# Permuted tokens, 512-column groups over all batches and a hand-set order in an attention and channel-mix kernel

## The chip, the cores and the metric

The kernel runs on one core of one Trainium2 chip. The metric is the device time of one execution in microseconds (us). Most executions of one kernel agree within about 1%; a run more than 1.5% above the fastest run of the same kernel is marked slow, and only fast runs enter a comparison. PE is the matrix engine (PEld its weight loads), DVE the vector engine, ACT the scalar engine, POOL the engine that issues the casting loads, SP the one that issues the stores.

## The reference

```python
def _attn_ref(q, k, v, g_norm):                       # (8, 8, 576, 64): batch, head, token, dim
    kv = np.einsum('bhsd,bhse->bhde', k, v)
    out = np.einsum('bhsd,bhde->bhse', q, kv)
    rms = np.sqrt(np.mean(out * out, axis=-1, keepdims=True) + 1e-06)
    return out / rms * g_norm

def _moe_ref(x, mu_k, mu_r, w_k, w_v, w_r):           # x: (8, 576, 512); w_k (512, 1024), w_v (1024, 512), w_r (512, 512)
    x_prev = x shifted by one token, zero first
    xk = mu_k * x + (1 - mu_k) * x_prev
    xr = mu_r * x + (1 - mu_r) * x_prev
    k = np.maximum(xk @ w_k, 0)
    return sigmoid(xr @ w_r) * ((k * k) @ w_v)
```

The output of the attention, heads side by side, is the x of the channel mix. All is float32 outside; inside, the matmuls are bf16.

## The kernel before

One batch at a time, 576 tokens in four chunks of 128 and one of 64. While the channel mix of batch b runs, the attention of batch b+1 is put in at four places. Every load moves pieces of one head of one token, 64 elements. The order of instructions is left to a scheduler, which here kept close to the order of the program.

```python
    def emit_partC_st(a):                       # the normalization's 1/rms, by Ln and Exp
        for half in range(2):
            ps_st = ps_tile("ps_st", [H, SH])
            # ... four matmuls with a selector sum the squares of each head ...
            nc.scalar.activation(out=st_sb, in_=ps_st, func=AF.Ln, bias=eps[:H], scale=1.0 / HD)
            nc.scalar.activation(out=rrms[half], in_=st_sb, func=AF.Exp, scale=-0.5)

    for b in range(B):
        a = b + 1
        emit_loads(b + 2)
        if a < B: emit_partA(a)                 # transposes of q (ps_qt), copies by ACT
        emit_moe_km(b, 0); emit_moe_km(b, 1)    # ps_km, relu by ACT, square by DVE
        emit_moe_r(b)                           # ps_r, sigmoid by ACT
        if a < B: emit_partB(a)                 # kv (ps_kv), u = q kv (ps_u), copies by ACT, squares by DVE
        emit_moe_v(b, 0)                        # ps_v, product by DVE, store
        if a < B: emit_partC_st(a)              # above
        emit_moe_v(b, 1)
        if a < B: emit_partC_rr(a)              # ps_rr, products, difference, blends by DVE
        emit_moe_v(b, 2); emit_moe_v(b, 3); emit_moe_v(b, 4)
```

Of the kernel before, what the change touches and what calls it, by code (L numbers as in the profile page):

```python
# [15 lines left out]
def kernel(  # L17
# [13 lines left out]
    nc = tc.nc  # L31
# [4 lines left out]
    SH = S // 2  # L36
    NHP = H // 2
    NFC = F // 128

    tok_chunks = []  # L40
    t0 = 0
    while t0 < S:
        sz = min(128, S - t0)
        tok_chunks.append((t0, sz))
        t0 += sz
    NTC = len(tok_chunks)

    const = ctx.enter_context(tc.tile_pool(name="const", bufs=1))
    stage = ctx.enter_context(tc.tile_pool(name="stage", bufs=4))
    inp = ctx.enter_context(tc.tile_pool(name="inp", bufs=3))  # L50
    work = ctx.enter_context(tc.tile_pool(name="work", bufs=1))
    psum = ctx.enter_context(tc.tile_pool(name="psum", bufs=8, space=bass.MemoryType.PSUM))

    def ps_tile(name, shape, dtype=FP32):
        return psum.tile(shape, dtype, tag="ps", name=name)

    ident = const.tile([128, 128], BF16, name="ident")
    ident4 = const.tile([4, 4], FP32, name="ident4")
    make_identity(nc, ident)
    make_identity(nc, ident4)  # L60
# [4 lines left out]
    sel8 = const.tile([128, 8 * NHP], BF16, name="sel8")  # L65
    nc.vector.memset(sel8, 0.0)
    for hp in range(NHP):
        for e in range(2):
            nc.vector.memset(sel8[64 * e:64 * e + 64, 10 * hp + e:10 * hp + e + 1], 1.0)

    selg = const.tile([H, C], BF16, name="selg")
    nc.vector.memset(selg, 0.0)
    g_row = g_norm.rearrange("(o d) -> o d", o=1)
    for h in range(H):
        nc.gpsimd.dma_start(out=selg[h:h + 1, HD * h:HD * h + HD], in_=g_row)

    kv_sb = [const.tile([128, 128], BF16, name=f"kv{hp}") for hp in range(NHP)]
    for hp in range(NHP):
        nc.vector.memset(kv_sb[hp], 0.0)

    mu_raw_k = const.tile([NHP, 128], FP32, name="mu_raw_k")
    mu_raw_r = const.tile([NHP, 128], FP32, name="mu_raw_r")
    nc.sync.dma_start(out=mu_raw_k, in_=moe_mu_k.rearrange("(j p) -> j p", p=128))
    nc.sync.dma_start(out=mu_raw_r, in_=moe_mu_r.rearrange("(j p) -> j p", p=128))
    mu_sb = const.tile([128, 2 * NHP], FP32, name="mu_sb")
    for idx, raw in enumerate((mu_raw_k, mu_raw_r)):
        ps_mu = ps_tile("ps_mu", [128, NHP])
        nc.tensor.matmul(ps_mu, raw, ident4, start=True, stop=True)
        nc.scalar.copy(out=mu_sb[:, NHP * idx:NHP * idx + NHP], in_=ps_mu)

    w_k_sb = [const.tile([128, F], BF16, name=f"w_k{i}") for i in range(NHP)]
    w_r_sb = [const.tile([128, C], BF16, name=f"w_r{i}") for i in range(NHP)]
    w_v_sb = [const.tile([128, C], BF16, name=f"w_v{i}") for i in range(NFC)]
    w_stage = {}

    def emit_w_dma(tag, src, i, ncols):
        st = stage.tile([128, F], FP32, tag="stage", name=f"stg_{tag}{i}")
        nc.sync.dma_start(out=st[:, :ncols], in_=src[128 * i:128 * i + 128, :])
        w_stage[(tag, i)] = st[:, :ncols]

    def emit_w_cast(tag, dst_list, i, eng):
        src = w_stage.pop((tag, i))
        if eng is nc.scalar:
            eng.copy(out=dst_list[i], in_=src)
        else:
            eng.tensor_copy(out=dst_list[i], in_=src)

    qT_sb = [work.tile([128, S], BF16, name=f"qT{hp}") for hp in range(NHP)]
    xT = [work.tile([128, S + 1], BF16, name=f"xT{hp}") for hp in range(NHP)]
    for hp in range(NHP):  # L110
        nc.vector.memset(xT[hp][:, 0:1], 0.0)
    uT_sb = {}
    sqT = {}
    for hp in range(NHP):
        for half in range(2):
            uT_sb[(hp, half)] = work.tile([128, SH], BF16, name=f"uT{hp}_{half}")
            sqT[(hp, half)] = work.tile([128, SH], BF16, name=f"sqT{hp}_{half}")
    st_sb = work.tile([H, SH], FP32, name="st_sb")
    rrms = [work.tile([H, SH], BF16, name=f"rrms{i}") for i in range(2)]
    xkT = [work.tile([128, S], BF16, name=f"xkT{hp}") for hp in range(NHP)]  # L120
    xrT = [work.tile([128, S], BF16, name=f"xrT{hp}") for hp in range(NHP)]
    dT_dve = work.tile([128, S], BF16, name="dT_dve")
    sqkT = [work.tile([128, S], BF16, name=f"sqkT{fc}") for fc in range(NFC)]
    relu_tmp = [work.tile([128, SH], BF16, name=f"relu{fc}") for fc in range(NFC)]
    sig = [work.tile([128, C], BF16, name=f"sig{ci}") for ci in range(NTC)]
    out_sb = [work.tile([128, C], FP32, name=f"out_sb{ci}") for ci in range(NTC)]

    inp_tiles = {}

    def emit_loads(b):  # L130
        if b >= B:
            return
        d = {}
        for name, src in (("q", q), ("k", k), ("v", v)):
            srcb = src[b].transpose([1, 0, 2])
            lst = []
            for ci, (t0, sz) in enumerate(tok_chunks):
                t = inp.tile([128, C], BF16, tag=f"{name}{ci}", name=f"{name}{ci}")
                nc.gpsimd.dma_start(out=t[:sz], in_=srcb[t0:t0 + sz])
                lst.append(t)  # L140
            d[name] = lst
        inp_tiles[b] = d

    def emit_partA(a):
        tiles = inp_tiles[a]["q"]
        for hp in range(NHP):
            ps_qt = ps_tile("ps_qt", [128, S], BF16)
            for ci, (t0, sz) in enumerate(tok_chunks):
                nc.tensor.transpose(  # L149
                    ps_qt[:, t0:t0 + sz],  # L150
                    tiles[ci][:sz, 128 * hp:128 * hp + 128],
                    ident[:sz, :sz],
                )
            nc.scalar.copy(out=qT_sb[hp], in_=ps_qt)  # L154

    def emit_partB(a):
        ktiles = inp_tiles[a]["k"]
        vtiles = inp_tiles[a]["v"]
        for hp in range(NHP):
            ps_kv = ps_tile("ps_kv", [128, 128])  # L160
            for ci, (t0, sz) in enumerate(tok_chunks):
                nc.tensor.matmul(  # L162
                    ps_kv,
                    ktiles[ci][:sz, 128 * hp:128 * hp + 128],
                    vtiles[ci][:sz, 128 * hp:128 * hp + 128],
                    start=(ci == 0),
                    stop=(ci == NTC - 1),
                )
            for e in range(2):
                sl = slice(64 * e, 64 * e + 64)  # L170
                nc.vector.tensor_copy(out=kv_sb[hp][sl, sl], in_=ps_kv[sl, sl])  # L171
        for half in range(2):
            for hp in range(NHP):
                ps_u = ps_tile("ps_u", [128, SH])
                nc.tensor.matmul(
                    ps_u,
                    kv_sb[hp],
                    qT_sb[hp][:, SH * half:SH * half + SH],
                    start=True,
                    stop=True,  # L180
                )
                ut = uT_sb[(hp, half)]
                nc.scalar.copy(out=ut, in_=ps_u)  # L183
                nc.vector.tensor_mul(out=sqT[(hp, half)], in0=ut, in1=ut)

    def emit_partC_st(a):
        for half in range(2):
            ps_st = ps_tile("ps_st", [H, SH])
            for hp in range(NHP):
                nc.tensor.matmul(  # L190
                    ps_st,
                    sel8[:, 8 * hp:8 * hp + 8],
                    sqT[(hp, half)],
                    start=(hp == 0),
                    stop=(hp == NHP - 1),
                )
            nc.scalar.activation(out=st_sb, in_=ps_st, func=AF.Ln,  # L197
                                 bias=eps[:H], scale=1.0 / HD)
            nc.scalar.activation(out=rrms[half], in_=st_sb, func=AF.Exp, scale=-0.5)  # L199

    def emit_blend(hp, eng, dT):
        xcur = xT[hp][:, 1:S + 1]
        xprev = xT[hp][:, 0:S]
        eng.tensor_tensor(out=dT, in0=xcur, in1=xprev, op=ALU.subtract)
        eng.scalar_tensor_tensor(out=xkT[hp], in0=dT, scalar=mu_sb[:, hp:hp + 1],  # L205
                                 in1=xprev, op0=ALU.mult, op1=ALU.add)
        eng.scalar_tensor_tensor(out=xrT[hp], in0=dT, scalar=mu_sb[:, NHP + hp:NHP + hp + 1],
                                 in1=xprev, op0=ALU.mult, op1=ALU.add)
# [142 lines left out]
```

## Time and profile before

| | before |
|---|---|
| time, median | 316.5 us |
| first channel-mix matmul | 46.9 us; in a row, without waits, from 54.0 |
| period of a middle batch | 34.2 us (83.5 to 117.7) |
| PE busy | 80% of the span |
| ACT table loads | 41, each 1.283 us |

The page's lines below give each engine's busy time and its share of the span, then rows of 40 equal slices of the span (a digit is tenths; PEclk is the clock granted to PE in tenths of full speed), then one DMA queue's packets, and two groups of ACT's instructions with their count, busy us and mean ns.

```profile
PE 251.3 (80%) x1508; PEld 137.9 (44%) x1508; DVE 186.6 (59%) x479; ACT 173.5 (55%) x343; POOL 110.4 (35%) x144
PE   1023568995999599987999599959998699959994
PEclk9999956998999979997999899997999799988999
q0 software_dynamic: 112768, 14.16, 74.3%
L199 ACT ACT_TABLE_LOAD x16 | 20.5, 1283 | 0.3
L197 ACT ACT_TABLE_LOAD x16 | 20.5, 1283 | 0.3
```

PE is the busiest engine, but slices with a 5 or 6 come back (the 10th, 14th, 23rd, 27th, 32nd and 36th), about one period of 34.2 us apart (4.3 slices; one dip is split between the 18th and 19th), and the clock dips to 7 or 8 in the same slice or the next. The chain of waits shows why. Each line has the start, the length and what the chain was on:

```profile
99.92 0.40 ACT uT_0_149 L183
...
102.45 1.28 ACT L197
103.75 0.49 ACT st_sb L197
104.30 1.26 issue
105.55 0.44 ACT rrms_166 L199
106.01 1.28 ACT L197
107.31 0.49 ACT st_sb L197
107.82 1.28 ACT L199
109.11 0.45 ACT rrms_167 L199
109.61 1.01 PE ps_rr L214 x7
110.62 7.09 PE ps_v L261 x24
```

From 99.9 to 109.6 the span hangs on ACT. Four of the pieces are loads of an activation table (the lines with an ACT line number and no tile; the second of the four, at 104.30, goes under "issue"). In this program Ln and Exp are taken from different tables: each switch between them has a load of 1.28 us (16 loads at the line of Ln, 16 at that of Exp). PE has only the matmuls of two chunks to do meanwhile. The stretches below (length, then busy us of each engine, granted clock, DMA) show a whole period and its end:

```profile
83.50:117.70 34.20, 30.41 (x189) 16.77 (x189) 22.61 (x58) 21.15 (x42) 12.58 (x15) 0.95 1.04 94
110.00:117.70 7.70, 7.70 (x31) 3.03 (x29) 7.70 (x16) 0.00 (x0) 0.00 (x0) 0.78 0.57 45
```

### The profile page before, as it was taken

To read this page: it belongs to the slowest core of one execution; us is meant where nothing else is said; L and a number is where in the kernel's file an instruction comes from. 1 tells how busy PE (TensorE), PEld (TensorE's weight loads), DVE (VectorE), ACT (ScalarE), POOL (GpSimd) and SP (SyncE) were. 2 spreads that over 40 slices of the span, in tenths; PEclk is the share of its full clock that TensorE was granted. 3 is DMA by queue.
4 is the path that set the end of the run, shared out by engine and by line. 5 is a ranking of instruction groups with operands and counts; after the bars stand their busy time and mean duration, and the time that the engine had idled before them with its cause. 6 is when DMAs were issued, how large, how long until landed. Compare 5 with 4: busy or idle time off the path is not lost.

```text
span 314.5 us, 4358 instructions
## 1 busy us (share of the span) xinstructions
PE 251.3 (80%) x1508; PEld 137.9 (44%) x1508; DVE 186.6 (59%) x479; ACT 173.5 (55%) x343; POOL 110.4 (35%) x144
## 2 busy tenths in 40 slices
PE   1023568995999599987999599959998699959994
PEld 1012234652574237532665247424754266425641
DVE  3100559565974398366856497439836686649712
ACT  2211861975277907792397627790688339760830
POOL 7589989999533705090406400000000000000000
PEclk9999956998999979997999899997999799988999
DMA  7999999999991959299496901010200010010213
GB/s 211 274 185 146 142 212 105 141 142 185 168 117 12 164 41 148 14 113 106 86 75 45 173 34 53 0 67 2 85 2 33 33 70 17 0 69 18 67 41 111
DMA packets 120359, 29.14 MB, mean 93 GB/s; under 512 B 113672, under 2 KB 113680, under 8 KB 120336
## 3 DMA queue, kind: packets, MB, share of 16 engines
q0 software_dynamic: 112768, 14.16, 74.3%
q1 hardware_dynamic: 7568, 14.69, 13.7%
q8 instruction: 12, 0.20, 0.2%
q14 instruction: 11, 0.09, 0.1%
HBM read 33.56 MB, written 9.44 MB: 137 GB/s over the span
## 4 chain that ended last, share of the span: by engine, by line
PE 60%; ACT 21%; DMA 8%; issue 4%; DVE 4%; POOL 2%; DVEq 0%; POOLq 0%
PE ps_km L232 19%; PE ps_v L261 18%; PE ps_r L248 11%; ACT L197 7%; PE ps_kv L162 4%; PE ps_qt L149 4%; ACT L199 3%; DMA q_203<-in_q_dram 3%; PE ps_rr L214 3%; DMA q_207<-in_q_dram 3%; ACT st_sb L197 3%; DMA v_231<-in_v_dram 2%; ACT rrms_167 L199 1%; ACT rrms_166 L199 1%; ACT uT_0_149 L183 1%
## 5 line engine op out<-in xcount | busy, mean ns | idle before, releaser
L154 ACT COPY qT_137<-ps_qt 128x576 bf16<-128x576 bf16 x8 | 5.1, 639 | 62.8 <-PE ps_qt L149 62.8
L232 PE MATMUL ps_km<-xkT_168,w_k_121 128*128 128x288 bf16 x128 | 36.7, 296 | 0.3 <-DVE xT_143 L221 0.3
L232 PE MATMUL ps_km<-xkT_169,w_k_122 128*128 128x288 bf16 x128 | 36.4, 296 | 0.3 <-DVE xkT_169 L205 0.3
L232 PE MATMUL ps_km<-xkT_170,w_k_123 128*128 128x288 bf16 x128 | 34.1, 289 | 0.0
L171 DVE CAST kv_102<-ps_kv 64x64 bf16<-64x64 f32 x16 | 3.5, 222 | 49.5 <-PE ps_kv L162 49.4
L214 PE MATMUL ps_rr<-rrms_167,selg 8*128 8x288 bf16 x32 | 9.4, 314 | 26.2 <-ACT rrms_167 L199 26.2
L232 PE MATMUL ps_km<-xkT_171,w_k_124 128*128 128x288 bf16 x128 | 28.6, 286 | 0.7 <-DVE xkT_171 L205 0.6
L240 ACT ACTIVATE relu_185<-ps_km 128x288 bf16<-128x288 f32 x16 | 7.2, 451 | 29.3 <-PE ps_km L232 29.3
L214 PEld LDWEIGHTS <-selg 8*128 8x128 bf16 x64 | 6.1, 96 | 38.0 <-issue 36.5
L199 ACT ACT_TABLE_LOAD x16 | 20.5, 1283 | 0.3
L197 ACT ACT_TABLE_LOAD x16 | 20.5, 1283 | 0.3
L221 DVE TENSOR_TENSOR xT_141<-uT_1_151,ps_rr 128x288 bf16<-128x288 bf16 x8 | 3.7, 458 | 24.9 <-PE ps_rr L214 24.9
L261 PE MATMUL ps_v<-w_v_129,sqkT_177 128*128 128x512 bf16 (+1 forms) x40 | 17.1, 428 | 0.0
L261 PE MATMUL ps_v<-w_v_130,sqkT_178 128*128 128x512 bf16 (+1 forms) x40 | 16.9, 424 | 0.0
L261 PE MATMUL ps_v<-w_v_131,sqkT_179 128*128 128x512 bf16 (+1 forms) x40 | 16.9, 423 | 0.0
L261 PE MATMUL ps_v<-w_v_132,sqkT_180 128*128 128x512 bf16 (+1 forms) x40 | 16.9, 423 | 0.0
L261 PE MATMUL ps_v<-w_v_133,sqkT_181 128*128 128x512 bf16 (+1 forms) x40 | 16.9, 423 | 0.0
L261 PE MATMUL ps_v<-w_v_134,sqkT_182 128*128 128x512 bf16 (+1 forms) x40 | 16.9, 423 | 0.0
L261 PE MATMUL ps_v<-w_v_135,sqkT_183 128*128 128x512 bf16 (+1 forms) x40 | 16.8, 421 | 0.0
L261 PE MATMUL ps_v<-w_v_136,sqkT_184 128*128 128x512 bf16 (+1 forms) x40 | 16.1, 403 | 0.0
L248 PE MATMUL ps_r<-w_r_125,xrT_172 128*128 128x512 bf16 (+1 forms) x40 | 15.4, 384 | 0.0
L248 PE MATMUL ps_r<-w_r_126,xrT_173 128*128 128x512 bf16 (+1 forms) x40 | 15.2, 379 | 0.0
(429 smaller groups left out, 754.0 us busy)
## 6 DMA issues: line engine op xcount, KB each, us to landing
out_dram<-out_sb_198 SPq DMA_DIRECT2D x8, 256.0 KB, 3.1
out_dram<-out_sb_199 SPq DMA_DIRECT2D x8, 256.0 KB, 3.3
out_dram<-out_sb_200 SPq DMA_DIRECT2D x8, 256.0 KB, 2.0
out_dram<-out_sb_201 SPq DMA_DIRECT2D x8, 256.0 KB, 2.6
out_dram<-out_sb_202 SPq DMA_DIRECT2D x8, 128.0 KB, 2.4
stg_k_263<-in_moe_w_k_dram SPq DMA_DIRECT2D x1, 512.0 KB, 3.4
stg_k_266<-in_moe_w_k_dram SPq DMA_DIRECT2D x1, 512.0 KB, 5.1
stg_k_269<-in_moe_w_k_dram SPq DMA_DIRECT2D x1, 512.0 KB, 6.4
```

Source lines behind the costliest of these rows:

```text
L149: nc.tensor.transpose(ps_qt[:, t0:t0 + sz], tiles[ci][:sz, 128 * hp:128 * hp + 128], ident[:sz, :sz],)
L154: nc.scalar.copy(out=qT_sb[hp], in_=ps_qt)
L162: nc.tensor.matmul(ps_kv, ktiles[ci][:sz, 128 * hp:128 * hp + 128], vtiles[ci][:sz, 128 * hp:128 * hp + 128], start=(ci == 0), stop=(ci == ...
L171: nc.vector.tensor_copy(out=kv_sb[hp][sl, sl], in_=ps_kv[sl, sl])
L197: nc.scalar.activation(out=st_sb, in_=ps_st, func=AF.Ln, bias=eps[:H], scale=1.0 / HD)
L199: nc.scalar.activation(out=rrms[half], in_=st_sb, func=AF.Exp, scale=-0.5)
L214: nc.tensor.matmul(ps_rr, selg[:, 128 * hp:128 * hp + 128], rrms[half], start=True, stop=True,)
L221: nc.vector.tensor_mul(out=xT[hp][:, 1 + SH * half:1 + SH * half + SH], in0=uT_sb[(hp, half)], in1=ps_rr,)
L232: nc.tensor.matmul(ps_km, w_k_sb[cc][:, 128 * fc:128 * fc + 128], xkT[cc][:, SH * hk:SH * hk + SH], start=(cc == 0), stop=(cc == NHP - 1),)
L240: nc.scalar.activation(out=rt, in_=ps_km, func=AF.Relu)
L248: nc.tensor.matmul(ps_r[:sz], xrT[cc][:, t0:t0 + sz], w_r_sb[cc], start=(cc == 0), stop=(cc == NHP - 1),)
L261: nc.tensor.matmul(ps_v[:sz], sqkT[fc][:, t0:t0 + sz], w_v_sb[fc], start=(fc == 0), stop=(fc == NFC - 1),)
```

## The change

The intent as given: tokens permuted so that a load moves runs of 1.5 KB; channel mix in 9 groups of 512 columns over all batches instead of 8 batches of 576; an order set by hand, with the attention between the units of channel-mix matmuls. The core of the diff, cut:

```diff
-                nc.gpsimd.dma_start(out=t[:sz], in_=srcb[t0:t0 + sz])
+                    nc.gpsimd.dma_start(
+                        out=inp_tiles[(n, b)][:, hs, :],
+                        in_=src[n][b, hs].rearrange("h (p j) d -> p h (j d)", j=NJ),   # token = 6 p + j: runs of 6 tokens
+                    )
     ... weights: float32 loads on SP and casts on three engines -> casting loads on POOL's queue, behind batch 0 ...
+    ctx.enter_context(tc.manual_schedule())
     ... transposes, kv, u, stat and rr on parts of the PE array: 64 x 64 outputs, 32-row and 32-column tiles ...
+            if half == 1:
+                nc.scalar.preload_act_table_set("natural_log_exp_and_others")
+            nc.scalar.activation(out=ln, in_=ps, func=AF.Ln, bias=eps, scale=1.0 / HD)
+            nc.scalar.activation(out=st["rs"][:, cs], in_=ln, func=AF.Exp, scale=-0.5)
     ...
+    def front(b, g, slots):                     # after unit slots[i] of group g
+        at(g, slots[0], (a["kv"], [0, 1, 2, 3]))
+        for hp in range(NHP):
+            at(g, slots[1 + hp], (a["transposes"], hp))
+    def rest(b, g, s0):
+        for hp in range(NHP):
+            at(g, s0 + hp, (a["u"], hp), (a["squares"], hp))
+        at(g, s0 + 5, (a["stat"], 1), (a["stat"], 0))
+        at(g, s0 + 8, (a["xmul"], 1))
+        at(g, s0 + 9, (a["xmul"], 0))
+        at(g, s0 + 10, (a["diff"],))
+        for hp in range(NHP):
+            at(g, s0 + 11 + hp // 2, (a["blend"], xk, 0, hp))
+            at(g, s0 + 13 + hp // 2, (a["blend"], xr, NHP, hp))
+    front(1, 0, [0, 1, 2, 3, 4])
+    rest(1, 0, 5)
+    for b in range(2, B):
+        front(b, b - 2, [15, 16, 17, 18, 19])
+        rest(b, b - 1, 2)
```

A group has 20 units of four matmuls: 8 of k (ps_km), 4 of r (ps_r), 8 of v (ps_v); group 0 has r first.

## The prediction

> **What bounds it now.** The chain of waits gives PE 60% of the span, ACT 21%, loads 8%. Three parts:
> - Start, 54 us: the first channel-mix matmul (ps_km) starts at 53.96, after loads until 30.8 us, then attention of batch 0 through ACT and DVE. The loads move 128-byte pieces (112,768 packets); the timeline shows POOL issuing them without a break, 0.87 us for 1024 pieces, 0.71 for 512, 0.55 for one: issue is the limit.
> - Eight batches. In the chain ps_km takes 7.95 us, ps_r 4.43, ps_v 40 matmuls at 0.2215 = 8.87: 21.25 us. Attention's PE work is about 6.9 us (ps_qt 1.85, ps_kv 1.95, ps_u 1.1, ps_st and ps_rr 1 each). Yet the period is 34.2 us (83.47 to 117.71): about 5 us idle, since PE waits for an ACT chain (eight copies, then Ln, Exp, Ln, Exp with 1.28 us table loads), and some 1.5 us lost at a clock of 0.78 after it (stretches table, 110 to 117.7).
> - Tail 4.3 us.
>
> **Removed.** The 64-token fifth chunk, whose matmuls cost a full 0.22 us: 720 matmuls of 512 columns x 0.2215 = 159.5 us against 170, -10.5. The exposed chain: attention is spread between matmul units, so idle and throttle mostly go: about -38 us over seven batches. ACT table loads, 41 to about 17 (-31 us of ACT, off the critical path once attention is). Weight casts on three engines. Loads in 768-byte pieces become DMA-bound.
>
> **Added.** 48 transposes of 96 columns and 48 kv matmuls of 64 columns per batch, instead of 20 + 20 of 128. The trace shows 57 ns per load-and-matmul pair at 128 columns; I estimate 45 to 55 ns: 4.8 us against 3.8. ps_u, ps_st, ps_rr use part of the array each, so should overlap: about 1.7 us instead of 3.1. But changing the tile shape costs about 0.09 us: in ps_qt the step to 64 rows and back starts 0.15 and 0.13 us apart instead of 0.057. [...] About 24 changes per batch x 0.09 = 2 us. Sum about 8 us per batch, 56 for seven (before 48).
>
> **Start.** Batch 0 is 3.5 MB of reads, alone at first; POOL's pace before was 270 GB/s of reads, so I assume 300: q lands at about 14 us. Then transposes 3, u 3.5, stat 3, DVE products, difference and four xr blends 9: first ps_r at about 33 us. Then PE must wait for batch 1's k, v, q, queued behind 5.2 MB of weights: 12.3 MB / 300 GB/s puts q at about 43 us, hence about 5 us of stall in group 0.
>
> **Sum.** 33 + 5 + 159.5 + 56 + tail 3.5 + small waits 3 = 260 us. DVE (about 165 us) and ACT (about 145) stay under PE.
>
> Predicted 260 us, range 243 to 280. Chances: faster 0.97, within 2% 0.02, slower 0.01.
>
> **What would show it.** First ps_r near 33 us. PE 90% or more after 45 us, clock near 1.0. Wide matmuls 0.216 to 0.222 us apart. Group period about 25.5 us for middle groups, 17.7 for the last. PE's waits: batch 1's kin and qin in group 0, little later. About 17 table loads; about 20,000 packets.
>
> **What would make it wrong.** Narrow-tile pairs costing 80 to 100 ns (weight loads not hidden): +20 us. DVE falling behind between units 10 and 16 (12 us of its work against 7 of PE) so that PSUM buffers run out: +2 to 3 us a group. Loads faster than 300 GB/s: -8 us.

## The result, and the profile after

| | before | after |
|---|---|---|
| time, median | 316.5 us | 251.9 us |
| ratio, 95% interval | | 0.793 (0.790 to 0.797) |
| first channel-mix matmul | 46.9 us (in a row from 54.0) | 27.1 us |
| period in the middle | 34.2 us per 576 tokens | 24.5 us per 512 tokens |
| PE busy | 80% | 87% |
| ACT table loads | 41 | 16 |

A ratio is the mean time of one kernel's fast runs over that of the kernel before's in the same rounds, so it is not quite the ratio of the medians. Where I give a difference in us between two versions below, it is the difference of their ratios times 316.5 us.

The page after, the lines that answer to those above:

```profile
PE 218.7 (87%) x1746; PEld 93.2 (37%) x1746; DVE 154.6 (62%) x302; ACT 136.0 (54%) x252; POOL 23.6 (9%) x38
PE   0284369969998999899989998999899989999992
PEclk9997559995999999999999999999999999999999
q0 software_dynamic: 20960, 16.78, 44.1%
GB/s 82 182 208 207 203 203 204 203 81 54 206 182 0 42 183 226 2 45 179 230 2 55 206 197 0 56 114 0 3 83 85 4 0 85 87 9 159 1 55 113
```

PE's row stands at 8 or 9 from the 11th slice to the last but one, and the clock at 9 (90% or more) from the 11th on. The q0 packets fell from 112,768 to 20,960 (with the weights now among them). The last row counts written bytes: through slices 3 to 8 the loads write 203 to 208 GB/s, and since they turn float32 into bf16 they read about twice that (over the whole run 33.56 MB read from HBM against 16.78 MB that q0 wrote). The chain of waits in a middle group:

```profile
75.63 0.60 ACT relu L222
76.24 1.28 ACT L176
77.54 0.51 ACT ln L177
78.07 0.44 ACT rs L178
78.51 0.40 ACT ln L177
78.93 0.44 ACT rs L178
79.40 1.28 ACT L232
80.69 0.61 ACT sig L232
81.34 3.61 PE ps_v L242 x16
```

The chain still runs through the Ln and Exp step, but that step has one table load in place of four (the second one here, at 79.40, brings back the table of the sigmoid; the whole switch takes 1.3 us, from the end of the relu at 76.23 to Ln at 77.54), and PE had r units to do beside it: PE's own wait ahead of ps_v at 81.34 is 0.55 us (the timeline), where it was 3.3 us. The stretches show group 0, a middle group and one of the last two groups, which have no attention in them:

```profile
27.10:66.70 39.60, 33.94 (x305) 13.88 (x306) 21.36 (x40) 16.63 (x32) 3.83 (x5) 0.77 1.01 160
66.70:91.20 24.50, 23.79 (x210) 9.87 (x210) 19.94 (x38) 16.11 (x30) 2.31 (x3) 1.00 0.56 97
210.90:228.20 17.30, 17.30 (x82) 7.84 (x80) 8.66 (x17) 7.10 (x12) 0.00 (x0) 1.00 0.29 78
```

A middle group has 0.7 us of idle PE left; the next ones are the same to 0.1 us. Group 0 takes 39.6 us at a mean clock of 0.77. PE's timeline there, with the wait in brackets, shows the two waits inside it (the 3.49 us in the first line lie ahead of group 0):

```profile
27.12 2.79 PE L229 MATMUL ps_r<-w_r,xr 128*128 128x512 bf16 x4 [3.49 <-DVE xr L202]
33.18 1.49 PE L141 MATMUL ps_kv<-vin,kin 96*64 96x64 bf16 x48 [3.27 <-DMA vin<-in_v_dram]
...
53.94 0.39 PE L242 MATMUL ps_v<-w_v,sqk 128*128 128x512 bf16 x1 [1.95 <-DVE sqk L223]
```

The one at 33.18 is the wait for batch 1's loads. The one at 53.94 is a wait for the last square, whose relu stood in ACT's queue behind the whole Ln and Exp step: in ACT's timeline the table load starts at 49.80 and that relu at 52.84, with Ln, Exp, Ln and Exp between them.

The low clock in the second half of group 0 (0.51 from 55.8 to 62.7 us) belongs to this profile and need not come with the waits: in the profiles of e1_pieces, e3_bybatch, e5_statlate, e7_both and e8_best below the clock row stands at 9 there, and four wide matmuls between two visits of attention take 0.97 us in e1_pieces and e5_statlate (1.81 here at 56.9), in e1_pieces behind a wait for the last square as here (its chain goes through that square at 60.16 us). Ahead of the first ps_km the rows of those profiles say 9 as well, but matmuls are slow there as in this one (clock 0.50 from 21.7 to 38.8 us): four ps_r take 1.89 us at 34.60 here and at 43.10 in e1_pieces. From the first ps_km of group 0 to the first of group 1 it is 26.1 us in this profile and 23.4 us in that of e1_pieces, with the same order at full clock. So lengths of group 0 can be compared only from the first ps_km on, and between profiles with the same clock there.

So where did 65 us come from? The span before is 54 us until ps_km runs in a row, 256 us of batches and a tail of about 4 us. After, it is 27.1 us of start, 39.6 us of group 0, 144.3 us for six groups, 34.5 us for the last two and 4.7 us of tail. The profile alone cannot say which part of a many-part change bought what. The experiments can.

### The profile page after: what moved, and what is told of

Read it like the earlier page. It is cut to its first block, busy times and chain, and to the rows that moved or that the text cites. A ratio compares the mean times of both kernels' runs of the same rounds, so it can differ in the third digit from the quotient of the medians.

```text
span 250.2 us, 4403 instructions
## 1 busy us (share of the span) xinstructions
PE 218.7 (87%) x1746; PEld 93.2 (37%) x1746; DVE 154.6 (62%) x302; ACT 136.0 (54%) x252; POOL 23.6 (9%) x38
## 3 DMA queue, kind: packets, MB, share of 16 engines
q0 software_dynamic: 20960, 16.78, 44.1%
HBM read 33.56 MB, written 9.44 MB: 172 GB/s over the span
## 4 chain that ended last, share of the span: by engine, by line
PE 69%; ACT 15%; DMA 12%; issue 1%; DVE 1%; POOL 1%; DVEq 0%; POOLq 0%
PE ps_v L242 26%; PE ps_km L219 26%; DMA vin<-in_v_dram 9%; PE ps_r L229 5%; PE ps_qt L125 4%; PE ps_u L159 4%; ACT L176 4%; ACT L232 3%; PE ps_kv L141 3%; DMA kin<-in_k_dram 3%; ACT ln L177 3%; ACT rs L178 2%; ACT relu L222 2%; ACT sig L232 1%; DVE out_sb L247 1%
## 5 line engine op out<-in xcount | busy, mean ns | idle before, releaser
L242 PE MATMUL ps_v<-w_v,sqk 128*128 128x512 bf16 x288 | 70.0, 387 | 5.3 <-ACT sig L232 3.3
L219 PE MATMUL ps_km<-xk,w_k 128*128 128x512 bf16 x288 | 68.9, 380 | 0.0
L222 ACT ACTIVATE relu<-ps_km 128x512 bf16<-128x512 f32 x72 | 42.9, 597 | 28.9 <-PE ps_km L219 24.4
L223 DVE TENSOR_TENSOR sqk<-relu 128x512 bf16<-128x512 bf16 x72 | 30.3, 425 | 35.5 <-ACT relu L222 35.3
L229 PE MATMUL ps_r<-w_r,xr 128*128 128x512 bf16 x144 | 37.3, 400 | 3.9 <-DVE xr L202 3.5
L242 PEld LDWEIGHTS <-sqk 128*128 128x128 bf16 x288 | 26.2, 98 | 37.7 <-issue 7.7
L219 PEld LDWEIGHTS <-w_k 128*128 128x128 bf16 x288 | 25.2, 98 | 32.3 <-issue 6.5
L247 DVE TENSOR_TENSOR out_sb<-ps_v,sig 128x512 f32<-128x512 f32 x36 | 24.2, 686 | 16.7 <-PE ps_v L242 16.7
L161 ACT CAST uT<-ps_u 128x288 bf16<-128x288 f32 x64 | 22.1, 413 | 0.0
L190 DVE TENSOR_TENSOR xT_133<-uT,ps_rr 128x288 bf16<-128x288 bf16 x32 | 12.3, 449 | 8.9 <-PE ps_rr L187 8.8
L190 DVE TENSOR_TENSOR xT_134<-uT,ps_rr 128x288 bf16<-128x288 bf16 x32 | 12.3, 449 | 6.7 <-PE ps_rr L187 6.7
L125 PEld LDWEIGHTS <-qin 96*64 96x64 bf16 x384 | 11.1, 119 | 14.3 <-issue 12.3
```

Of the source, the lines that this page charges most:

```text
L125: nc.tensor.transpose(ps[64 * e:64 * e + 64, NP * j:NP * j + NP], qin[:, 2 * hp + e, HD * j:HD * j + HD], ident[:NP, :NP],)
L161: nc.scalar.copy(out=st["uT"][:, hp, cs], in_=ps)
L190: nc.vector.tensor_mul(out=xT[:, hp, NP + HS * half:NP + HS * half + HS], in0=st["uT"][:, hp, cs], in1=pss[hp])
L219: nc.tensor.matmul(ps, w_k_sb[:, cc, 128 * fc:128 * fc + 128], xk[:, cc, G * g:G * g + G], start=(cc == 0), stop=(cc == NHP - 1))
L222: nc.scalar.activation(out=rt, in_=ps, func=AF.Relu)
L223: nc.vector.tensor_mul(out=sqk[g][:, fc, :], in0=rt, in1=rt)
```

## The experiments

Theory at the outset, from the prediction: the order set by hand hides the ACT chain and so makes the largest part of the gain; table loads matter little once attention is spread out. Rivals: the table loads themselves; the long load runs; the wide groups.

### One part undone at a time

**e1_pieces.** Tokens in natural order, loads in pieces of 64 elements, as before; all else as changed.

```diff
-                        in_=src[n][b, hs].rearrange("h (p j) d -> p h (j d)", j=NJ),
+                        in_=src[n][b, hs].rearrange("h (j p) d -> p h j d", j=NJ),
-            nc.vector.tensor_copy(out=xT[:, :, 1:NP], in_=xT[:, :, S:S + NP - 1])     # and in1 of diff and blend one column back
-            dst = out[b].rearrange("(p j) c -> j p c", j=NJ)[j, p:p + cnt]
+            dst = out[b][c:c + cnt]
```

> The changed kernel with tokens in their natural order: the loads go back to pieces of 64 elements (256 bytes read, 128 written), everything else stays. Theory (long runs matter only while loads bound the kernel, that is at the start): batch 1 lands some 9 us later than at 33 us, so +6 to +12 us (258 to 264), and the middle groups keep their period of 24.5 us. Rival (the long runs are a main cause of the gain): +20 us or more, with loads also late in the middle groups.

Measured: 256.1 us median, ratio 0.807 (0.802 to 0.813): 4.4 us slower than the change. The window of expectation began at 6. In the trace kv of batch 1 starts at 38.3 us (33.2 with long runs) and a middle group still takes 24.5 us (70.8 to 95.3), although the loads now are 118,419 packets in all against 26,771. The written rate during the start falls from about 204 to 140 to 180 GB/s in most slices. So the runs are worth something only where loads hold PE up, at the start; the rival falls.

**e2_place** and **e2b_place.** The old placement of the attention steps, in the changed kernel. The two are the same program.

```diff
-    front(1, 0, [0, 1, 2, 3, 4]) ... rest(b, b - 1, 2)
+    for b in range(1, B):
+        a, g = steps[b], b - 1
+        for hp in range(NHP):
+            at(*((g - 1, 19) if g else (0, 3)), (a["transposes"], hp))
+        at(g, 11, (a["kv"], [0, 1, 2, 3]))
+        for hp in range(NHP):
+            at(g, 11, (a["u"], hp), (a["squares"], hp))
+        at(g, 13, (a["stat"], 1), (a["stat"], 0))
+        at(g, 15, (a["xmul"], 1), (a["xmul"], 0), (a["diff"],))      # then the xk and xr blends, also at 15
```

> The changed kernel with the attention steps put where the kernel before has them (transposes ahead of the group, kv and u as a block after the last k or r unit, stat after v chunk 0, products, difference and blends after v chunk 1). Theory (the hand-set order carries the largest part of the gain): per group about 6 us of idle PE plus up to 2 us at a low clock, +40 to +56 us (292 to 308). Rival (the order is worth little; fewer and wider matmuls and table loads made the gain): under +10 us.

> The old placement of the attention steps in the changed kernel once more, since its four times fell into 258 and 264 to 266. If the order is worth about 6 us most fall near 258; if about 13, near 265. Theory: the middle period is 27.2 us in the profiled run against 24.5, seven times, of which the shorter group 0 gives some back, so most near 264.

Measured: of eight times three are fast (257.9, 258.1 and 255.9, mean 257.3 us) and five are marked slow (262.6 to 265.6). By the fast ones the old placement costs about 5 us over the changed kernel's median, where I expected 40 to 56; even the slow ones lie only 11 to 14 us above it. The theory I began with falls: with one table load in the Ln and Exp step, the old coarse placement hides nearly as much as the fine one. In the fast profile PE's remaining waits are 0.9 us a batch for the products that give PSUM buffers (where PE writes its results) back and 0.5 us for kv. The slow profile has the same waits, and a lower clock in its groups (0.94 on average against 1.00 in most groups of the fast one); since only slow runs show that, I draw nothing from it. My second expectation, that most runs fall near 264, came out as two and two and settles nothing.

**e3_bybatch.** Eight groups of one batch: k in halves of 288 columns, r and v in chunks of 128, 128, 128, 128 and 64 tokens.

```diff
-    G = 512
-    NG = B * S // G
+    G = S
+    NG = B
+        m = min(128, G - 128 * ci)               # in unit_r and unit_v; unit_k loops over two halves of 288
```

> The changed kernel with 8 groups of one batch each: k in halves of 288 columns, r and v in four chunks of 128 tokens and one of 64. Theory: wide matmul work rises from 155.5 to about 166 us, all on PE's critical path: +10 to +14 us (262 to 266). Rival (the waits between have room for it): under +3 us.

Measured: 256.8 us, ratio 0.809 (0.805 to 0.813): 4.9 us slower, between theory and rival. The extra matmul work is real: a batch takes 27.5 us in the middle and 20.8 us at the end without attention, so eight batches have 166 us of wide matmuls against 155. But only 4.9 of these 11 us show. In the middle a batch is 3.0 us longer than a group, for 3.5 us more of wide matmuls; PE's wait for ACT is 0.37 us there instead of 0.55. Group 0 is no longer than the change's (38.9 against 39.6 us), but this profile has the full clock from the first ps_km on and the change's has not, so how much of the rest its waits hide is not shown.

**e4_tables.** Only the preload line taken out.

```diff
-            if half == 1:
-                nc.scalar.preload_act_table_set("natural_log_exp_and_others")
```

> The changed kernel without the preload of the table that holds both Ln and Exp: 40 table loads instead of 16, 3.85 us more of ACT in each stat step. Theory (PE already waits 0.55 us a group for the sigmoid behind the stat step, so each added us of ACT there shows): +20 to +30 us (272 to 282). Rival (four PSUM buffers absorb it): under +6 us.

Measured: 291.9 us, ratio 0.920 (0.914 to 0.925): 40 us slower, more than the theory's 20 to 30. The chain of waits of this run:

```profile
107.97 0.60 ACT relu L220
108.58 1.28 ACT L175
...
110.40 1.28 ACT L176
...
112.15 1.28 ACT L175
...
113.97 1.28 ACT L176
...
115.72 1.28 ACT L230
117.02 0.61 ACT sig L230
117.66 4.43 PE ps_v L240 x10
```

Five table loads stand where the changed kernel has two. A period is 30.9 us (99.04 to 129.95) against 24.5: 6.4 us more for 3.85 us of loads. PE is idle for 5.3 us of such a period (0.7 in the change) and busy for 25.6 us (23.8 in the change) with the same matmuls. The stretches of the same run show the rest:

```profile
106.00:114.00 8.00, 5.13 (x32) 2.10 (x32) 3.04 (x8) 7.49 (x12) 0.00 (x0) 1.00 0.24 37
114.00:118.00 4.00, 2.01 (x10) 0.71 (x10) 2.24 (x7) 3.96 (x6) 0.00 (x0) 0.72 0.00 0
118.00:122.00 4.00, 4.00 (x10) 1.48 (x10) 1.96 (x3) 1.08 (x3) 0.00 (x0) 0.50 0.02 4
```

PE is idle for 4.9 of 12 us, in waits of at most 1.51 us, and then its clock is halved: between 118 and 122 us it does 10 wide matmuls at 0.44 us each, not 0.216. So here a wait for ACT is paid twice, once as a wait (4.6 us more of it in a period) and once as slow matmuls behind it (1.8 us); in the middle groups of the change, with 0.7 us of idle PE, the clock is 1.00. In the whole run the mean clock is 0.92.

### The same part alone, in the kernel before

**b1_tables** and **b2_tables** (the same program twice). One preload per batch ahead of Ln and Exp. So that the preload stays where it is put, ACT alone is held to the order of the program.

```diff
+    ctx.enter_context(tc.manual_schedule(engines={mybir.EngineType.Activation}))
     def emit_partC_st(a):
+        nc.scalar.preload_act_table_set("natural_log_exp_and_others")
         for half in range(2):
```

PE's and DVE's instructions are the same, one for one and in the same order, as in the kernel before. On ACT, besides 24 table loads gone, the four casts of w_r move behind the first Ln and Exp step.

> The kernel before with one table preload per batch ahead of Ln and Exp (17 table loads instead of 41); ACT keeps its program order so that the preload stays in place, PE's and DVE's orders are the same instruction for instruction. Theory (the table loads in the stat step are the largest single cause of the gain, also without the new order): 3 x 1.28 us leave the chain that PE waits for in each batch, and PE's clock holds: -27 to -40 us (277 to 290). Rival (the loads cost much only in the new order, which has little else to wait for): under -12 us.

> The kernel before with one table preload per batch once more, for a profile at full clock: 275 to 280 us, the period of a middle batch 29.3 us or less where it was 34.2, and no stretch of low clock in it. If the gain were made elsewhere (start or end), the period would stay near 34.

Measured: 277.5 us, ratio 0.870 (0.862 to 0.879), and 276.6 us, ratio 0.870 (0.862 to 0.879) the second time: 41 us faster than the kernel before, just above what the theory said. (One more run of b1_tables, 323.1 us, had a mean granted clock of 0.77; it is marked slow and not used.) The stretches of two periods of b2_tables:

```profile
74.20:103.40 29.20, 28.85 (x186) 16.32 (x188) 21.91 (x58) 17.30 (x39) 25.87 (x32) 1.00 2.16 171
103.40:132.50 29.10, 28.88 (x186) 16.34 (x188) 21.81 (x57) 17.30 (x39) 12.43 (x16) 1.00 1.09 102
```

The period is 29.1 us where it was 34.2, PE is idle for 0.3 us of it, and the clock is 1.00. Six periods of 5 us make 30 us. Most of the rest is the start: ps_km runs in a row from 45.3 us instead of 54.0; 3.85 us of these 8.7 are the loads in the Ln and Exp step of batch 0. In this run the last v load of batch 0 also landed 4 us earlier (26.8 instead of 30.8), which the moved casts may have caused; I did not test that. So some 36 of the 41 us are the table loads: all but the 4.9 us of the start that they do not explain.

### Undoing all but the preload

**e9_allthree.** The edits of e1, e2 and e3 together; preload, load order and the use of parts of the array kept.

> Natural token order, groups by batch and the old placement together, in the changed kernel with its table preload and its load order kept. Theory (the parts add up): +4.2, +4.9 and +6 to +13 over the changed kernel, 267 to 274, which is near the kernel before with the preload (277.5); the rest of the difference is the start. Rival (the parts hide each other's waits): under 263.

Measured: 285.5 us, ratio 0.898 (0.892 to 0.903): 33 us slower than the change, and slower than the kernel before with the preload. The parts neither add up (theory) nor hide each other (rival); together they cost more than twice the sum of the single ones, 4.4 + 5 + 4.9. A period is 30.4 us (107.0 to 137.4) where e3 alone has 27.5, and its chain goes through DVE's products, difference and blends straight to the first ps_km of the next batch. My reading, argued from these numbers and not tested further: each part undone alone is half hidden in a wait that stays (group 0, or the 0.55 us of a middle group); undone together, nothing is left to hide in.

### Can the remaining waits go?

**e5_statlate.** The Ln and Exp step behind the last unit whose relu or sigmoid PE needs (in group 0 one unit later, in middle groups four), and what follows by as much (the last blends at most to unit 19).

```diff
+    def rest(b, g, s0, st=5):                    # d = st - 5 is added to every later slot
-        at(g, s0 + 5, (a["stat"], 1), (a["stat"], 0))
+        at(g, s0 + st, (a["stat"], 1), (a["stat"], 0))
+    rest(1, 0, 5, st=6)   ...   rest(b, b - 1, 2, st=9)
```

> The changed kernel with the stat step of each batch behind the last k or r unit of its group, and the steps after it moved by as much. Theory (ACT does its work in program order, and the stat step stands ahead of a relu or sigmoid that PE needs): the 0.55 us wait of six groups and 4.7 us of ACT ahead of the last relu of group 0 go: -5 to -9 us (243 to 247). Rival (the wait moves on to the products and blends, which come later by four units): 0 or slower.

Measured: 250.7 us, ratio 0.789 (0.783 to 0.796): not told apart from the change. In the profile group 0 ends 5.5 us earlier (the first ps_km of group 1 at 61.2 instead of 66.7), but that is not all the edit: the clock recorded in this profile is 1.00 in group 0, where the change's was 0.77.

```profile
PEclk9999999999999999999999999999999999999998
```

From the first ps_km of group 0 to that of group 1 it takes 21.6 us, against 26.1 in the change's profile and 23.4 in that of e1_pieces at full clock: the edit itself is worth about 2 us there, which is the 1.95 us wait for the last square. And from group 1 until group 7 runs without a wait it takes 147.6 us instead of 144.3. Group 6 has no later batch's transposes to fill in, and behind it the chain goes through 3 us of blends that now come late (PE is idle for 2.2 us of them):

```profile
205.75 3.00 DVE xk L202 x4
...
208.80 6.42 PE ps_km L219 x29
```

**e6_order.** Batch 1 loaded ahead of w_k and w_v.

```diff
+    load_batch(1)
     nc.gpsimd.dma_start(out=w_k_sb, ...)
     nc.gpsimd.dma_start(out=w_v_sb, ...)
-    load_batch(1)
```

> The changed kernel with batch 1's k, v, q loaded ahead of w_k and w_v. Theory (at the start loads run at about 410 GB/s of reads without a break, and PE waits for batch 1 because 4.2 MB of weights stand ahead of it): kv of batch 1 can start at about 28 us instead of 33.2: -4 to -7 us (245 to 248). Rival (w_k and w_v then come too late for k at about 35 us): 0 to -2 us.

Measured: fast runs 245.0 and 248.1 us, ratio 0.775 (0.766 to 0.784): 6 us faster than the change, as the theory says. (Two runs are marked slow and not used: 248.7 us, only just over the limit, and 317.8 us with a mean clock of 0.69. The profile is of the latter, so I read the effect in the next. Its clock row stands at 6 from the 6th slice on, that of the slow run of b1_tables at 7 from the 7th; no run here shows why.)

**e7_both.** e5 and e6 together.

```diff
+    load_batch(1)                                # ahead of w_k and w_v
+    rest(1, 0, 5, st=6)   ...   rest(b, b - 1, 2, st=9)
```

> Both of the last two. Theory (they remove different waits): their sum, -9 to -16 us (236 to 243). Rival (one wait stands behind the other): no better than the better one.

Measured: 246.1 us, ratio 0.775 (0.770 to 0.781), the same as e6 alone, as the rival said, but not for its reason. Kv of batch 1 starts at 29.1 us with no wait for a load, where the change has it at 33.2 us, and from the first ps_km of group 0 to that of group 1 it takes 21.6 us, as in e5: both waits are gone. What e5 gains there it loses again at the late blends ahead of group 7 (3.0 us of them in the chain, from 201.7), as it did alone.

**e8_best.** The load order of e6; in group 0 the Ln and Exp step one unit later as in e5. In the middle groups u, the products and the blends come one unit earlier; the first half of the Ln and Exp step comes two units earlier and the second stays.

```diff
+    load_batch(1)                                # ahead of w_k and w_v
+        at(g, s0 + st[0], (a["stat"], 1))
+        at(g, s0 + st[1], (a["stat"], 0))
-    rest(1, 0, 5)   ...   rest(b, b - 1, 2)
+    rest(1, 0, 5, st=(6, 6))   ...   rest(b, b - 1, 1, st=(4, 6))
```

> The changed kernel with batch 1 loaded ahead of w_k and w_v, the stat step of group 0 behind its last relu, and in the middle groups u, stat and what follows one unit earlier, with the two halves of stat two units apart (so that ACT never holds a relu or sigmoid back for more than one table load, one Ln and one Exp). Theory: about 5.5 us in group 0, 4 to 5 at the start, and the 0.55 us wait of six groups: -10 to -14 us (238 to 242). Rival (DVE's products, one unit earlier, or the PSUM buffers bring a new wait): no better than 245.

Measured: 243.6 us, ratio 0.767 (0.764 to 0.770): 8.4 us faster than the change, 3.3%. It beats both kernels. The gain lies before the first middle group: that starts at 58.6 us instead of 66.7. (The recorded clock is 1.00 there in this profile, so some 2 to 3 of these 8 us are the clock and not a wait: 21.8 us from the first ps_km to that of group 1, against 26.1 at the low clock and 23.4 in e1_pieces at the full one.) A middle group still takes 24.6 us (58.57 to 83.18), and this is the rival's share:

```profile
68.52 1.83 PE ps_r L229 x8
70.62 1.55 DVE xT L190 x4
72.49 0.97 PE ps_r L229 x4
```

PE now reaches ps_rr before DVE has given PSUM buffers back, where before it waited for ACT. In this visit the four ps_rr take 0.94 us; 1.2 us earlier, with buffers free, they took 0.23. The wait changed its owner and stayed.

## Why the prediction was right or wrong

The time was right: 260 us with a range of 243 to 280, measured 251.9. In part that was luck, since errors cancel: the start is 6 us shorter than forecast, group 0 about 9 longer (39.6 against 17.7 + 8 + 5) and the six groups behind it about 9 shorter (144.3 against 6 x 25.5). The steps, one by one:

- **"POOL issuing ... is the limit", "Loads become DMA-bound".** Right that the loads got faster; that issuing was the limit before is not shown. POOL fell from 110.4 to 23.6 us busy. But e1_pieces, with pieces as before, writes 141 to 151 GB/s in slices 6 to 9 while POOL's row stands at 2 to 5; before, it is 141 GB/s from 54 to 59 us with POOL busy throughout. After, the DMA row stands at 9 in slices 2 to 8, and POOL's at 0 in three of them (4, 5 and 8). I assumed 300 GB/s of reads; the start writes 203 to 208 GB/s of bf16, so it reads about 408. How little the long runs were worth in time, e1_pieces shows: 4.4 us.
- **"first ps_r at about 33 us".** Measured 27.1. (The 53.96 us that the prediction gives for the first ps_km before is where ps_km runs in a row; the first starts at 46.91.) DVE's steps overlap: eight products take 3.0 us in a row, not 8 x 0.45 = 3.6; four xr blends 3.0, not 3.2; and ps_r starts with the first blend, not the last (the timeline).
- **"about 5 us of stall in group 0".** PE's idle time there is 39.6 - 33.9 = 5.7 us, but the number was met partly by luck: 3.3 us of it is for loads, and 1.95 us for a square behind the Ln and Exp step, which I had not foreseen. I also left out the clock, 0.77 on average in this profile and recorded as 1.00 in others, whose matmuls ahead of the first ps_km are as slow.
- **"I estimate 45 to 55 ns" for a narrow pair.** Mis-sized. 48 kv matmuls take 0.88 us (18 ns each), 12 transposes 0.38 us (32 ns each). In the trace the two matmuls of a pair of heads, which write different halves of the output's 128 partitions, start 3 ns apart, and the next two about 32 ns later. A weight load takes 98 ns for most of ps_qt in the kernel before and 119 to 128 ns on average for these, yet they start 18 to 32 ns apart: the risk of 80 to 100 ns a pair did not come. **"so should overlap"** held: the eight ps_st of a middle group start within 0.14 us (75.52 to 75.66), where before they took 0.86 (102.65 to 103.50). **"changing the tile shape costs about 0.09 us"** held: four wide matmuls between two visits of attention take 0.97 us where four in a row take 0.86 (6.91 for 32), 0.11 us more, and the step from the last wide matmul to the first of kv is 0.31 us (84.57 to 84.88) where two wide ones start 0.216 apart. Attention costs 24.5 - 17.3 = 7.2 us per middle group with the wait in it; I had said 8.
- **"720 matmuls of 512 columns ... -10.5".** Right as work (e3: 166 us against 155), wrong as time: undone alone it is worth 4.9 us.
- **"attention is spread between matmul units, so idle and throttle mostly go: about -38 us" and "ACT table loads, 41 to about 17 (-31 us of ACT, off the critical path once attention is)".** Here the reason was wrong, though the sum was right. That the range was met in spite of it is luck: one change held both the order and the preload. I credited the order with hiding the ACT chain and gave the table loads nothing. e2 shows that the order alone buys about 5 us; e4 and b1 show that the preload alone buys 36 to 40 us, in either kernel. Spread out or not, the Ln and Exp step stands in ACT's queue ahead of sigmoids that ps_v waits for, so the loads stay on the critical path. With the preload, going from Ln to Exp and back needs no second load (76.24 to 79.37 us of the profile after; 16 loads with it, 40 without). I had counted the loads and did not put them on the chain.
- **"DVE falling behind"** was named as a risk. In the change the wait left in a middle group is ACT's; e8 removed it and met DVE's, and the group stayed at 24.6 us.

So of 65 us, 36 to 40 hang on the one line of preload. The other parts together make the rest. The three of them that I undid cost about 5 us each singly and 33 all at once, so no share can be given to one alone. The casting loads of the weights, the use of parts of the array and the load order at the start were never undone, so what they bring is not shown.

## What to carry to other kernels

When one engine works in program order, as ACT does in these traces (the relu at 52.84 us behind 3.0 us of table load, Ln and Exp), ask for every slow step on it which later result of that engine the bottleneck needs: a step that is "not on the critical path" is on it if a needed result queues behind it. Look at table loads first: here Ln and Exp in turn cost a load of 1.28 us per switch, and the set that holds both cost one per step, but was taken only where the preload asked for it (40 loads in e4_tables without that line, 16 with it). To find out what a many-part change bought, take single parts out of the new kernel and also put single parts into the old one, since parts taken out singly can hide in each other's waits (here 14.3 us singly, 33 together).
